# Top-k attention and a low-rank mixer: scales in one transfer a head, transposes of u two shares later, border work of batches 1 and 2 moved

## The chip, the cores and the metric

The kernel runs on one core of one Trainium2 chip. The metric is the device time of one execution in microseconds (us), the median over several. A core has five engines with queues of their own, each worked off in order: TensorE (PE, matrix products; its weight loads are listed as PEld), VectorE (DVE), ScalarE (ACT), GpSimd (POOL) and SyncE (SP). SP and ACT also issue the DMAs of this kernel; an issue holds the issuing queue.

## The reference

Eight batches, eight heads, 576 positions, 64 channels a head. For each head

```
scores = q k^T / 8                      (576 x 576)
keep the 32 largest of each row, softmax over them, x_head = attn v
x = heads side by side                  (576 x 512)
u = x + V^T U^T x     (mixing over the 576 positions, rank 32)
out = u + relu(u w1) w2                 (512 -> 2048 -> 512)
```

All is float32. U, V, w1 and w2 arrive as 64-bit numbers and are turned to 32 bits on the chip.

## The kernel before, in words

**Units of work.** Heads go in pairs `g` (four pairs a batch, 32 in all). The 576 query rows of a pair are four full tiles `t` = 0..3 of 128 rows, each with both heads side by side, and a tail tile `t` = 4 (`NT`) with 64 rows of each head on 128 partitions. A loop over steps `n` (L1182) takes one tile a step; from pair 4 (`NPAIR`, the first of batch 1 counted from 0, "batch 2" in the title's count) tile 3 and the tail share a step. Code before L1264 serves the first batch, the code from L1264 the other seven.

**A tile's way.** PE makes the scores (L336, L368), ACT copies them to SBUF (L381, L401, L404). To find the 32nd largest of a row, a tile is folded from pair 5 on: POOL adds the two halves as bits (L432), DVE takes the larger of each couple (L434, it reads one half straight from PSUM), POOL subtracts to get the smaller (L435). DVE then picks eights: L487 and L485 on the small half, L502, L515 and L520 on the large one. ACT and POOL turn everything under the threshold into a huge negative number (L546, L549, L550), ACT takes the exponential and its row sums `den` (L439, L560). From pair 6 DVE transposes in 32x32 blocks (L576), SP writes them to DRAM (`away`, L582), ACT issues the read back as `PT` (L591); earlier pairs, and all tails, are transposed on PE (L612, L617). PE multiplies with v (L688, L691, L662), ACT copies the result to `XT` (L700, L669), which has channels on partitions and positions along the row.

**The scales.** From pair 4 on the division by the row sums comes after that: `inverse` (L621) takes 1/`den` on DVE (L629, L631) and SP writes it to a DRAM tile `rd` of nine rows of 128 (L635): row 2t+h for tile t and head h, row 8 for the tail (64 of each head). `scale` (L639) reads it back spread over partitions, the 576 scales of head h on each of the 64 partitions of its half, with four DMAs a pair issued by ACT: per head one of 64x4x128 (L645) and one of 64x64 (L649). `mixed` (L703) then forms u = XT * scale on POOL: two products of 128x256 (L719) and one of 128x64 (L720).

**The mixing.** `mixed` is a generator, one stretch of which runs at each `fill()`. A step has eight such calls ("shares"). After the products it yields twice; PE then transposes u (four 128x128 at L725, the tail at L738) and ACT copies the result to `X` (L729, L739). It then waits until the next step has issued its values (L740 to L743), after which PE forms U^T x (L750), ACT copies (L758), PE multiplies with V (L762), ACT copies (L777), POOL adds to u (L778). The last pair is called with a fixed wait (`wait` = 5) instead. For pair 4 POOL also clears 64 rows of `X` (L736) here.

**The MLP.** `fill()` also takes from a queue of matmuls of the batch before, as many as a fixed share allows: L810 (first layer) with the ReLU copy L823 on ACT, L828 (second layer), then L839 on ACT and L840 on POOL, transposes L852, copies L854 and the store L858. The order on every engine is thus written down by the program; nothing is decided at run time.

**Parameters.** `next_params` (L218) brings in one block of weights a call: SP loads the raw words (L154), ACT makes three passes (L176, L177, L180), DVE one (L188), POOL two (L189, L191).

**The border.** Pair 4 is not folded, pair 5 is the first that is. The first fold's DVE and POOL part (`split`: L434, L435) was held back by `bound` until after the last selection of the step. Unfolded tiles write their first round of L515 to a `place`: for tiles of two heads a buffer with the tag `upper`, the tag that a fold's result uses too.

Of the kernel before, what the change touches and what calls it, by code (L numbers as in the profile page):

```python
# [26 lines left out]
def kernel(  # L27
# [106 lines left out]
    def at(t):  # L134
        return slice(OFF[t], OFF[t] + rows(t))

    def half(h):
        return slice(h * D, (h + 1) * D)
# [315 lines left out]
    def front(tiles):  # L454

        lanes = []
        for g, t in tiles:  # L460
            if t == 0:
                dens[g] = small.tile([P, 2 * NT + 1], F32, tag="den", name="den", bufs=3)
            S2, den = S2s.pop((g, t)), dens[g]
            early, pooled, gaps = ways(g, t)
            n = S2.shape[1]
            fold_of = folds.pop((g, t), None)
            for c in (1, 0) if n == 2 else (0,):
                slot = c if n == 2 or len(tiles) == 1 else 2
                lanes.append((
                    slot,  # L470
                    S2[:, c],
                    den[:, 2 * t + c : 2 * t + c + 1],
                    [a[:, c] for a in fold_of] if fold_of else None,
                    "early" if c in early else "pooled" if c in pooled else "gap" if c in gaps else "",
                ))
        W = len(lanes)
        first = small.tile([P, 3, 8], F32, tag="first", name="first", bufs=3)
        nmax = small.tile([P, 3], F32, tag="nmax", name="nmax", bufs=4)
        curs, places, ms = {}, {}, {}
        halves = [(lane[0], *lane[3]) for lane in lanes if lane[3]]  # L480
        for at_, step in ((0, 0), (0, 1), (8, 0)):
            for slot, upper, lower in halves:
                spot = upper[:, HALF + at_ : HALF + at_ + 8]
                if step:
                    nc.vector.match_replace(lower, spot, lower, NEG)  # L485
                else:
                    nc.vector.max(spot, lower)  # L487
        for slot, chunk, _, fold_of, _ in lanes:
            if fold_of:
                curs[slot] = fold_of[0]  # L490
            else:
                curs[slot] = chunk
                if slot == 2:
                    places[slot] = attn.tile([P, S], F32, tag="tplace", name="place", bufs=1)
                else:
                    places[slot] = attn.tile(
                        [P, 2, HALF + TOPK // 2], F32, tag="upper", name="upper"
                    ).rearrange("p c n -> p (c n)")[:, 0:S]
            ms[slot] = first[:, slot]
        order = [lane[0] for lane in lanes]  # L500
        for c in order:
            nc.vector.max(ms[c], curs[c])  # L502
        yield
        for i in range(1, TOPK // 8):
            if i == 1:
                nc.scalar.mul(nmax[:, 0:W], first[:, 0:W, 0], -SCALE)
                Es = {}
                for c, chunk, _, _, way in lanes:
                    if way == "early":
                        Es[c] = attn.tile([P, S], F32, tag="E", name="E")  # L510
                        weigh(chunk, Es[c], nmax[:, c : c + 1])
            for c in order:

                nxt = places.pop(c, curs[c])
                nc.vector.match_replace(nxt, ms[c], curs[c], NEG)  # L515
                curs[c] = nxt
            m8 = small.tile([P, 3, 8], F32, tag="m8", name="m8", bufs=4)
            for c in order:
                ms[c] = m8[:, c]
                nc.vector.max(ms[c], curs[c])  # L520
            yield
        for c, chunk, total, _, way in lanes:
            if way == "pooled":
                gap = attn.tile([P, S], F32, tag="E", name="E")
                nc.gpsimd.tensor_scalar(gap, chunk, ms[c][:, 7:8], NEG, ALU.is_lt, ALU.mult)
                nc.gpsimd.tensor_tensor(chunk, chunk, gap, ALU.add)  # L526
        for c, chunk, total, _, way in lanes:
            if way == "early":
                nc.vector.scalar_tensor_tensor(
                    out=chunk,  # L530
                    in0=chunk,
                    scalar=ms[c][:, 7:8],
                    in1=Es[c],
                    op0=ALU.is_ge,
                    op1=ALU.mult,
                    accum_out=total,
                )
        if t == NT:
            del qkTs[g]
        yield  # L540
        gaps = [lane for lane in lanes if lane[4] == "gap"]
        if gaps:
            slots = [lane[0] for lane in gaps]
            lo, hi = min(slots), max(slots) + 1
            least = small.tile([P, 3], F32, tag="least", name="least", bufs=3)
            nc.scalar.mul(least[:, lo:hi], m8[:, lo:hi, 7], WIDEN)  # L546
            for c, chunk, *_ in gaps:
                gap = attn.tile([P, S], F32, tag="E", name="E")
                nc.scalar.activation(gap, chunk, AF.Relu, bias=least[:, c : c + 1], scale=-WIDEN)  # L549
                nc.gpsimd.tensor_tensor(chunk, chunk, gap, ALU.subtract)  # L550
            yield
        rest = [lane for lane in lanes if lane[4] != "early"]
        if len(gaps) > 1:
            c, chunk, total, *_ = rest.pop(0)
            weigh(chunk, chunk, nmax[:, c : c + 1], total)
            yield
        for c, chunk, total, *_ in rest:
            weigh(chunk, chunk, nmax[:, c : c + 1], total)
        if t == NT and g != NPAIR - 1:
            nc.scalar.activation(den, den, AF.Identity, bias=eps)  # L560
        yield
# [77 lines left out]
    def scale(g):  # L639

        rd = scales.pop(g)
        sc = attn.tile([P, S], F32, tag="scale", name="scale", bufs=1)
        scales[g] = sc
        for h in range(2):
            nc.scalar.dma_start(  # L645
                sc[half(h), 0:MAIN].rearrange("p (t n) -> p t n", t=NT),
                rd[0 : 2 * NT].rearrange("(t h) n -> h t n", h=2)[h : h + 1].to_broadcast([D, NT, P]),
            )
            nc.scalar.dma_start(  # L649
                sc[half(h), MAIN:S], rd[2 * NT : 2 * NT + 1, half(h)].to_broadcast([D, TAIL])  # L650
            )

    def values(g, t):
# [49 lines left out]
    def mixed(g, wait, lag=0):  # L703
# [7 lines left out]
        uT = uTs[b][:, gi]  # L711
        if g >= NPAIR:
            sc = scales.pop(g)
            pairs_ = [
                a[:, 0:MAIN].rearrange("p (b n) -> p b n", b=2) for a in (XT, sc)
            ]
            ends = [uT[:, OFF[t] : OFF[t] + 2 * P] for t in (0, 2)]
            for i, end in enumerate(ends):
                nc.gpsimd.tensor_tensor(end, pairs_[0][:, i], pairs_[1][:, i], ALU.mult)  # L719
            nc.gpsimd.tensor_tensor(uT[:, at(NT)], XT[:, MAIN:S], sc[:, MAIN:S], ALU.mult)  # L720
            yield
            yield
        tp = ps_t.tile([P, NT, P], F32, tag="tp", name="tp")
        for t in range(NT):
            nc.tensor.transpose(  # L725
# [4 lines left out]
        if g < NPAIR:  # L730
            X4 = X4.rearrange("p t (h d) -> p t h d", h=2)
            den4 = den[:, 0 : 2 * NT].rearrange("p (t h) -> p t h ()", h=2)
            nc.gpsimd.tensor_tensor(X4, X4, den4.to_broadcast([P, NT, 2, D]), ALU.mult)
        else:
            if g == NPAIR:
                nc.gpsimd.memset(X[TAIL:P, NT, :], 0.0)  # L736
            tp = ps_t.tile([P, P], F32, tag="tp", name="tp")
            nc.tensor.transpose(tp[0:TAIL], uT[:, at(NT)], ident)  # L738
            nc.scalar.copy(X[0:TAIL, NT, :], tp[0:TAIL])  # L739
# [20 lines left out]
        for chunks, (lo, hi) in zip(PARTS, SPAN):  # L760
# [15 lines left out]
            else:  # L776
                nc.scalar.copy(sc[:, lo:hi], up[:, 0 : hi - lo])  # L777
                nc.gpsimd.tensor_tensor(uT[:, lo:hi], uT[:, lo:hi], sc[:, lo:hi], ALU.add)  # L778
            yield
        if gi == NPAIR - 1:  # L780
            fillers.append(closing(b) if b == B - 1 else mlp(b))

# [399 lines left out]
    for n in range(STEPS + 2):  # L1182
# [103 lines left out]
        if n < STEPS and n - 2 >= ALONE and len(tiles(n - 2)) > 1:  # L1286
            scale(steps[n - 2][0][0])
        next(here, None)
        next_params(1)
        fill()  # L1290
        if n >= STEPS:
            if n == STEPS:
# [1 line left out]
                scale(NP - 1)  # L1294
            weighted(n - 2)
        next(here, None)
        bound = tiles(n + 1)[:1] == [(NPAIR + 1, 0)]
        if not bound:
            for tile_ in tiles(n + 1):
                split(*tile_)  # L1300
        fill()
        next(here, None)
        if bound:
            for tile_ in tiles(n + 1):
                split(*tile_)
        for tile_ in tiles(n - 1):
            if shared(*tile_):
                blocks(*tile_)
# [5 lines left out]
                coming = loading(g + 2) if g + 2 < NP else iter(())  # L1314
            next(coming, None)
        next(ready, None)
        if t != 0:
            next_params(1)
        next(here, None)
        fill()  # L1320
# [36 lines left out]
```

## Time and profile before

| | |
|---|---|
| median of 3 runs | 1680.57 us (1680.2 to 1681.1) |
| the profiled execution | 1681.84 us, of which the span from first to last instruction is 1679.8 us |
| mean granted TensorE clock | 0.967 of full speed |
| busy: PE, DVE, ACT, POOL | 1571.6, 1547.1, 991.1, 1000.2 us |
| scale DMAs on ACT | 56 of 128 KB (L645, median 622 ns to issue) and 56 of 16 KB (L649, 627 ns) |
| products of u | 56 of 128x256 (L719, 740 ns), 28 of 128x64 (L720, 332 ns) |
| copies to X | 28 at L729 (586 ns), 28 at L739 (258 ns) |

How to read it: "busy" is time in which an engine executes, not time in which it decides the end. A wait row reads "engine line of the waiter <- engine line of the releaser: us in total, times, longest". In a timeline the columns are start, length, engine, line, operation and shape; a bracket gives the idle time before and who ended it. x counts instructions: a float32 matmul is two, a transpose one. Ends of matmuls are modelled, starts are not.

### The profile page before, as it was taken

The page shows a single profiled execution, that of the slowest core. Times are in us where ns is not written, and L with a number is a line of the kernel's source. Part 1 is how long each engine was busy: PE and PEld are TensorE (multiplying, and loading weights), DVE is VectorE, ACT ScalarE, POOL GpSimd, SP SyncE. Part 2 cuts the span into 40 slices and gives each one's busy share as a digit, 9 for nine tenths or more (in the row PEclk, how much of TensorE's full clock was granted, in tenths as well). Part 3 has the DMA queues.
Part 4 walks back from the last instruction along what each step waited for, and adds up shares of the span by engine and source line. Part 5 has one row for each costly group of instructions (what it writes and reads, how often), then busy time and mean ns, then how long its engine had stood idle before and what let it go on. Part 6 is the DMA issues. An engine that isn't in the chain of part 4 may idle for free.

```text
span 1679.8 us, 30303 instructions
## 1 busy us (share of the span) xinstructions
PE 1571.6 (94%) x9638; PEld 1183.9 (70%) x9638; DVE 1547.1 (92%) x4393; ACT 991.1 (59%) x2475; POOL 1000.2 (60%) x853
## 2 busy tenths in 40 slices
PE   4667698999899999999999999999999999999999
PEld 2444466687667786778777887778777887778776
DVE  7999998999999999999999999999999999994452
ACT  4888788665665556565655656565655656564320
POOL 4778668755666565666566565656666565653620
PEclk7787799999999999999999999999999999999999
DMA  3323232255555555555455455555555555543001
GB/s 87 94 76 97 62 94 73 63 135 132 134 128 135 127 142 132 139 127 138 121 134 137 124 146 132 137 128 136 126 130 136 126 149 132 131 120 110 10 1 28
DMA packets 295631, 189.42 MB, mean 113 GB/s; under 512 B 178768, under 2 KB 279984, under 8 KB 295472
## 3 DMA queue, kind: packets, MB, share of 16 engines
q1 hardware_dynamic: 259728, 117.62, 30.2%
q10 hardware_dynamic: 35744, 69.88, 13.7%
q8 instruction: 76, 1.25, 0.3%
q14 instruction: 83, 0.68, 0.1%
HBM read 116.49 MB, written 70.91 MB: 112 GB/s over the span
## 4 chain that ended last, share of the span: by engine, by line
PE 58%; DVE 25%; POOL 5%; DMA 4%; ACT 3%; issue 2%; SPq 2%; ACTq 0%; DVEq 0%; POOLq 0%
PE mm L828 17%; PE mm L810 16%; DVE m L520 7%; DVE upper L515 7%; PE sc L336 5%; PE O L691 5%; PE mm L904 3%; DVE first L502 2%; DVE y L576 2%; DVE upper L487 2%; PE sc L904 2%; PE tp L904 2%; DMA ld<-in_k_dram 2%; POOL uT L719 2%; PE up L762 1%
## 5 line engine op out<-in xcount | busy, mean ns | idle before, releaser
L550 POOL TENSOR_TENSOR Ssb<-Ssb,E 128x576 f32<-128x576 f32 x243 | 339.9, 1419 | 248.3 <-ACT E L549 247.8
L810 PE MATMUL mm<-uT,w 128*128 128x320 f32 (+1 forms) x1792 | 461.7, 410 | 2.4 <-ACT hT L823 2.0
L828 PE MATMUL mm<-hT,w 128*128 128x320 f32 (+1 forms) x1792 | 462.1, 407 | 0.0
L810 PEld LDWEIGHTS mm<-uT,w 128*128 128x128 f32 x1792 | 335.4, 191 | 103.0 <-issue 11.6
L828 PEld LDWEIGHTS mm<-hT,w 128*128 128x128 f32 x1792 | 332.3, 190 | 93.0 <-issue 10.2
L520 DVE MAX8 m<-upper 128x8 f32<-128x304 f32 (+1 forms) x780 | 367.3, 512 | 0.7
L515 DVE MATCH_REPLACE8 upper<-m,upper 128x304 f32<-128x304 f32 (+1 forms) x520 | 259.9, 507 | 0.0
L432 POOL TENSOR_TENSOR lower<-Ssb 128x576 uint32<-128x576 uint32 x108 | 152.6, 1413 | 139.1 <-ACT Ssb L381 52.2
L439 ACT ACTIVATE Ssb<-Ssb,nmax 128x576 f32<-128x576 f32 x258 | 201.4, 783 | 17.6 <-POOL Ssb L526 9.9
L435 POOL TENSOR_TENSOR lower<-lower,upper 128x576 uint32<-128x576 uint32 x108 | 153.1, 1418 | 74.2 <-DVE upper L434 72.6
L336 PE MATMUL sc<-qkT 64*128 64x288 f32 (+1 forms) x1056 | 179.0, 461 | 11.0 <-ACT Ssb L390 7.8
L487 DVE MAX8 upper<-lower 128x8 f32<-128x288 f32 x432 | 172.3, 440 | 10.7 <-POOL lower L435 10.7
L549 ACT ACTIVATE E<-Ssb,least 128x576 f32<-128x576 f32 x243 | 176.2, 769 | 4.2
L381 ACT COPY Ssb<-sc 128x576 f32<-128x576 f32 x216 | 127.6, 643 | 71.4 <-PE sc L336 71.4
L576 DVE STREAM_TRANSPOSE y<-Ssb 128x512 f32<-128x512 f32 (+1 forms) x312 | 153.9, 545 | 0.0
L823 ACT ACTIVATE hT<-mm 128x320 f32<-128x320 f32 (+1 forms) x224 | 91.9, 411 | 102.1 <-PE mm L810 100.9
L691 PE MATMUL O<-PT,va 128*64 128x128 f32 x2048 | 144.6, 285 | 0.0
L336 PEld LDWEIGHTS sc<-qkT 64*128 64x128 f32 (+1 forms) x1056 | 95.9, 197 | 51.7 <-issue 17.1
L691 PEld LDWEIGHTS O<-PT,va 128*64 128x64 f32 x2048 | 113.4, 141 | 16.4 <-issue 2.0
L700 ACT COPY XT<-O 128x128 f32<-128x128 f32 x128 | 33.8, 264 | 111.3 <-PE O L691 103.8
L515 DVE MATCH_REPLACE8 upper<-first,upper 128x304 f32<-128x304 f32 x216 | 97.7, 460 | 0.0
L485 DVE MATCH_REPLACE8 lower<-upper,lower 128x288 f32<-128x288 f32 x216 | 94.1, 444 | 0.0
(264 smaller groups left out, 2258.3 us busy)
## 6 DMA issues: line engine op xcount, KB each, us to landing
away<-y SPq DMA_DIRECT2D x416, 144.0 KB
PT<-away ACTq DMA_DIRECT2D x104, 576.0 KB
raw<-in_moe_w_ch_dram SPq DMA_DIRECT2D x32, 512.0 KB
va<-in_v_dram SPq DMA_DIRECT2D x64, 128.0 KB
out_dram<-ob SPq DMA_DIRECT2D x59, 128.0 KB
scale<-rd ACTq DMA_DIRECT2D x56, 128.0 KB
ld<-in_q_dram SPq DMA_DIRECT2D x108, 64.0 KB
ld<-in_k_dram SPq DMA_DIRECT2D x108, 64.0 KB
```

The lines of the kernel that those rows point to most:

```text
L336: nc.tensor.matmul(out, lhsT=qkT[half(h), 0, cols(t)], rhs=qkT[half(h), 1, lo:hi], start=True, stop=True,)
L435: nc.gpsimd.tensor_tensor(bottom, bottom, top.bitcast(U32), ALU.subtract)
L439: nc.scalar.activation(E, chunk, AF.Exp, bias=nmax, scale=SCALE, accum_out=total)
L487: nc.vector.max(spot, lower)
L515: nc.vector.match_replace(nxt, ms[c], curs[c], NEG)
L520: nc.vector.max(ms[c], curs[c])
L549: nc.scalar.activation(gap, chunk, AF.Relu, bias=least[:, c : c + 1], scale=-WIDEN)
L550: nc.gpsimd.tensor_tensor(chunk, chunk, gap, ALU.subtract)
L576: nc.vector.transpose(y[:, :, i * NT : i * NT + c].rearrange("p r c j -> p c r j"), E2[:, a : a + c * P].rearrange("p (c r j) -> p c r j", ...
L691: nc.tensor.matmul(O[half(h)], lhsT=va[:, h, j, :], rhs=PT[:, NT * h + j], start=False, stop=(j == NT - 1),)
L810: nc.tensor.matmul(ph[:, 0:w], lhsT=first_layer(cc, f), rhs=uT[:, cc, lo:hi], start=(cc == 0), stop=(cc == NC - 1),)
L828: nc.tensor.matmul(po[:, 0:w], lhsT=w2[:, f, c * P : (c + 1) * P], rhs=hTs[f][:, 0:w], start=(f == 0), stop=(f == NF - 1),)
```

## The change

1. **Scales.** `den` of pairs from 4 on is laid out head by head: column 5c+t for head c, so that columns 0 to 3 are head 0, column 4 the tail of both, 5 to 8 head 1. In `rd` the 576 scales of a head now lie in one run, those of head 1 from the middle of row 4. `scale` reads each with one DMA of 64 rows of 576 numbers: two DMAs a pair. The tile becomes 64 columns wider; head 0 has its tail behind, head 1 ahead, so the tail product is two of 64x64 on half the partitions each, in place of one of 128x64.
2. **Transposes.** After the products `mixed` yields four times, not twice, except for the last pair.
3. **Border.** `bound` goes; the first fold's second part stands at its usual place. The `place` buffers of that one step come from the idle tiles `scale` and `PTt`, not from `upper`. The call of `next_params` at that step goes, and one is added in the step of pair 5, tile 0. The clearing of 64 rows of `X` moves from pair 4's mixing to the end of pair 3's.

```diff
+                spot = CH * c + t if g >= NPAIR else 2 * t + c
-                    den[:, 2 * t + c : 2 * t + c + 1],
+                    den[:, spot : spot + 1],
...
+                elif (g, t) == (NPAIR, NT):
+                    places[slot] = attn.tile([P, TAIL + S], F32, tag="scale", name="place", bufs=1)[:, 0:S] if slot else (
+                        attn.tile([P, NT + 1, P], F32, tag="PTt", name="place", bufs=1)
+                    ).rearrange("p c n -> p (c n)")[:, 0:S]
...
-        sc = attn.tile([P, S], F32, tag="scale", name="scale", bufs=1)
+        sc = attn.tile([P, TAIL + S], F32, tag="scale", name="scale", bufs=1)
+        flat = rd.rearrange("r n -> () (r n)")
         for h in range(2):
             nc.scalar.dma_start(
-                sc[half(h), 0:MAIN].rearrange("p (t n) -> p t n", t=NT),
-                rd[0 : 2 * NT].rearrange("(t h) n -> h t n", h=2)[h : h + 1].to_broadcast([D, NT, P]),
-            )
-            nc.scalar.dma_start(
-                sc[half(h), MAIN:S], rd[2 * NT : 2 * NT + 1, half(h)].to_broadcast([D, TAIL])
+                sc[half(h), (1 - h) * TAIL : (1 - h) * TAIL + S],
+                flat[:, h * S : (h + 1) * S].to_broadcast([D, S]),
             )
...
-            nc.gpsimd.tensor_tensor(uT[:, at(NT)], XT[:, MAIN:S], sc[:, MAIN:S], ALU.mult)
-            yield
-            yield
+            for h in range(2):
+                a = (1 - h) * (TAIL + MAIN)
+                nc.gpsimd.tensor_tensor(
+                    uT[half(h), at(NT)], XT[half(h), MAIN:S], sc[half(h), a : a + TAIL], ALU.mult
+                )
+            for _ in range(4 if wait is None else 2):
+                yield
...
-            if g == NPAIR:
-                nc.gpsimd.memset(X[TAIL:P, NT, :], 0.0)
...
+        if g == NPAIR - 1:
+            nc.gpsimd.memset(X[TAIL:P, NT, :], 0.0)
...
-        next_params(1)
+        border = g == NPAIR and t == NT - 1
+        if not border:
+            next_params(1)
...
-        bound = tiles(n + 1)[:1] == [(NPAIR + 1, 0)]
-        if not bound:
-            for tile_ in tiles(n + 1):
-                split(*tile_)
+        for tile_ in tiles(n + 1):
+            split(*tile_)
         fill()
         next(here, None)
-        if bound:
-            for tile_ in tiles(n + 1):
-                split(*tile_)
...
-        if t != 0:
+        if t != 0 or g == NPAIR + 1:
             next_params(1)
```

More of the change, by code (lines that the diff above doesn't have):

```diff
@@ L713, in mixed @@
             sc = scales.pop(g)
-            pairs_ = [
-                a[:, 0:MAIN].rearrange("p (b n) -> p b n", b=2) for a in (XT, sc)
-            ]
+            main = sc[:, TAIL : TAIL + MAIN]
+            pairs_ = [a.rearrange("p (b n) -> p b n", b=2) for a in (XT[:, 0:MAIN], main)]
             ends = [uT[:, OFF[t] : OFF[t] + 2 * P] for t in (0, 2)]
```

## Prediction

> **What bounds the kernel now.** I read the busy time by windows first, cut at the period at which the timeline repeats (189.2 us, one batch), then the waits of DVE and PE, then timelines at the two places that these name.
>
> Busy time by windows (length, then busy and instructions of PE, PEld, DVE, ACT, POOL, then clock and DMA):
>
> ```profile
> core 0: us, PE busy (x) PEld busy (x) DVE busy (x) ACT busy (x) POOL busy (x), PEclk, DMA share, GB/s
> 741.93:931.13 189.20, 187.59 (x1189) 143.13 (x1189) 186.21 (x567) 112.25 (x286) 113.86 (x96) 1.00 0.54 133
> 336.00:552.73 216.73, 209.21 (x1322) 157.96 (x1321) 216.56 (x661) 129.92 (x331) 132.25 (x111) 0.98 0.53 133
> ```
>
> From 552 us to the last attention step at 1514 every batch looks like the first row: PE and DVE both nearly full. Between 336 and 552 (second row) DVE has 0.2 us idle in 217: there it alone sets the pace, and nothing that PE saves counts. ACT and POOL are at 60%.
>
> Waits of DVE, 336 to 1536 us:
>
> ```profile
> DVE upper L434 <- ACT Stail L401: 10.3, 9, 1.7
> DVE upper L487 <- POOL lower L435: 6.2, 7, 1.9
> ```
>
> These 16.5 us are nearly all that DVE loses in the stretch: each batch once 1.6 us at L434 and about 1.2 at L487. L401 copies scores that PE has just made, so the first row says that PE is late. PE waits for nothing there but the products of u:
>
> ```profile
> 756.66 0.44 PE L725 MATMUL tp<-ident,uT 128*128 128x128 f32 x2 [0.26 <-POOL uT L719]
> 757.35 0.44 PE L725 MATMUL tp<-ident,uT 128*128 128x128 f32 x2 [0.26 <-POOL uT L719]
> 757.63 0.30 PE L738 MATMUL tp<-ident,uT 128*64 128x128 f32 x1
> 757.78 2.54 PE L810 MATMUL mm<-uT,w 128*128 128x256 f32 x11
> ```
>
> That is PE's timeline at one pair. The last pair is one without the wait:
>
> ```profile
> 1551.29 0.60 PE L725 MATMUL tp<-ident,uT 128*128 128x128 f32 x4
> 1551.72 0.27 PE L738 MATMUL tp<-ident,uT 128*64 128x128 f32 x1
> 1551.83 2.54 PE L828 MATMUL mm<-hT,w 128*128 128x256 f32 x11
> ```
>
> From the first transpose to the next matmul it takes 0.54 us there and 1.12 here: 0.58 lost inside the group (ends are modelled, so the bracket shows less; starts count). Before it, twelve L810 from 753.55 last 3.11 us, where the last pair's eight take 1.84, 0.23 each: 0.35 more. The four pairs of this batch lose 0.93, 0.66, 0.97 and 0.98 in this way, **3.5 us a batch**. So PE needs 189.2 - 3.5 = 185.7 us a batch and DVE 186.2: PE bounds, and DVE is only 0.5 us behind it.
>
> The second wait of DVE, timeline of ACT, POOL and DVE:
>
> ```profile
> 790.65 0.62 ACTq L645 DMA_DIRECT2D scale<-rd  x1
> 791.31 0.63 ACTq L649 DMA_DIRECT2D scale<-rd  x1
> 791.97 0.62 ACTq L645 DMA_DIRECT2D scale<-rd  x1
> 792.63 0.62 ACTq L649 DMA_DIRECT2D scale<-rd  x1
> 793.30 0.20 ACT L506 ACTIVATE nmax<-first 128x2 f32<-128x2 f32 x1 [1.65 <-DVE m L520]
> 793.41 0.35 ACT L839 COPY oT<-mm 128x256 f32<-128x256 f32 x1
> 793.84 0.73 POOL L840 TENSOR_TENSOR oT<-oT,uT 128x256 f32<-128x256 f32 x1 [3.29 <-ACT oT L839]
> 794.53 1.42 POOL L435 TENSOR_TENSOR lower<-lower,upper 128x576 uint32<-128x576 uint32 x1
> 795.99 0.82 DVE L487 MAX8 upper<-lower 128x8 f32<-128x288 f32 x2 [0.96 <-POOL lower L435]
> ```
>
> Four issues hold ACT for 2.6 us; the copy L839 stands behind them, POOL's add L840 behind that, L435 behind it, and DVE waits. Around 602 us one issue lasts 1.54 us and the same chain costs DVE 1.85.
>
> **The change, part by part.** *Scales.* Two of four issues go: 1.31 us of ACT a pair (two at 0.62 to 0.63 and their spacing). In the chain above L839 could start at 792.1 (its matmuls end at 792.2), 1.2 us earlier, more than the 0.96 waited; at 602 us, without the third and fourth issue, about 2.1, more than 1.85. So the L487 waits go: **-6.2**. What an issue of 64 rows of 2304 bytes costs is not in the trace: below by the read of `PT` (L591, 128 rows of 4608 bytes, 0.33 us), above by L645's 0.62; I take 0.62. Its landing has cover: the last scale packet of the issues from 743.4 ends at 748.3, and L719 begins at 755.87, so 7.6 us later would still do. The Trainium skill (Perfetto Trace Analysis, DMA Optimizations) speaks against merging: split transfers may let work start sooner. With 7.6 us to spare that is worth nothing here, and by that rule too the sum would stay. The tail product becomes two: at most 2 x 0.33 for 0.33 on POOL (below, two of half the cost, nothing); L435 follows directly, ends at 758.95, and L487 takes its result at 759.76, so 0.33 fits in 0.8; without that cover it would be 0.33 x 28 = 9 us.
>
> *Transposes.* In PE's order they move three or four matmuls down (two instructions each, 0.22 us at 256 columns, 0.27 at 320), some 1.65 us past the place where they would start unhindered. At 756.66 that place is 756.31, so 757.96. L719 ends its second product at 757.25, the tail products end by 757.9, and the tail is transposed 0.44 after the first: all is there, with 0.4 us to spare. Group and copies end 0.7 us later than now, since the waits inside go. What is queued behind the copies on ACT: L546 and L549 of the same step, then L550 on POOL. In the tightest of the four pairs (804 us) ACT afterwards idles 3.88 us and POOL 4.16, which hides 0.7. On PE two matmuls (1.08 us) follow before the next user of the same PSUM buffer in one pair in four (L852), against a copy of 0.59: covered, else 0.5 a batch. L750 keeps its place. So PE gets 3.5 us a batch, and the L434 waits go: **-10.3**. What is late next: DVE itself. Its need of 186.2 stands 0.5 above PE's, and two engines that close hinder each other; `PT` is no obstacle, as L688 comes 6 to 9 us after its issue here and 4.5 to 5 where DVE set the pace without a loss. I leave **+5** (1 us a batch; ends 0, and 9, half of PE's saving).
>
> *Border.* Timeline of DVE, waits only:
>
> ```profile
> 250.24 0.82 DVE L487 MAX8 upper<-lower 128x8 f32<-128x288 f32 x2 [1.31 <-POOL lower L435]
> 261.98 0.21 DVE L629 RECIPROCAL upright<-den 128x9 f32<-128x9 f32 x1 [2.19 <-ACT den L560]
> 275.03 0.43 DVE L188 TENSOR_SCALAR w<-w 128x512 uint32<-128x512 uint32 x1 [2.80 <-ACT w L176]
> 289.55 0.82 DVE L487 MAX8 upper<-lower 128x8 f32<-128x288 f32 x2 [2.94 <-POOL lower L435]
> ```
>
> L434 moves ahead of three L515 and three L520 (4.2 us), so POOL, idle for 6.3 us there, has L435 done long before L487: 1.31 goes. PE's wait of 2.17 us for L434 at 248.66 goes too. One L188 (1.14 us) moves from 238 to behind L631, into the slack before the next L487. But L629 waits for a chain over L550, L439 and L560 that starts at the last L520, and that comes only some 0.4 us sooner; with one parameter's two POOL passes (2.6 us) out of its way I count 1.7 at 262. At 275 ACT is behind the four scale issues: 1.3 more. The 2.94 stays, as POOL and DVE move together. **-3.0**, from 0 (the chain does not move) to -4.9 (the 1.9 us at L434 at 331 goes as well). The cleared rows: POOL now waits for pair 3's last use (L766, done about 209.8) in front of an L189 that ran at 207.23; the next use of POOL is at 214.07 after 4.18 us idle, and the block whose load SP issues behind it (209.92) is first read at 218.86. Free; without cover 2.6. The later parameter block has 29 us to its first use. The clock: in the windows 248.3 to 251.7 and 425.8 to 432.6 the granted clock is 0.50, after PE idled 2.17 and 3.08 us. The Trainium skill (TensorE: Matmul & The Clock Gate, What's actually happening) has half clock only after an idle window of about 3.4 us, so by it the shorter wait would cost no clock. By the rows both did; but DVE sets the pace at both, so I add nothing for it.
>
> *Sum.* -3.0 - 6.2 - 10.3 + 5 = -14.5 against the profiled execution's 1681.84 us: 1667.3. The median was 1.27 lower, so **1666 us**.
>
> **Rivals.** (a) *Half of it*: the transposes still meet a late product (POOL's queue slides with ACT's), or PE meets a new wait, and only L487 and the border's 1.3 at the scale issues remain: 7.5, giving 1673. For it: the margin is 0.4 us. (b) *No change*: PE's wait moves into waiting for `PT` or for L434, and DVE's into another of POOL's results; 0 to 3 us, 1680. Against it: the windows 336 to 552, where DVE ran without such waits. (c) *Slower*: copies L729 and L739 reach ACT 0.7 us later and delay L546, L549, L550 and so POOL's L435 in each of 28 pairs: 28 x 0.7 = 19.6, less 6.2 and 3.0, is +10, 1691. It decides once L435 is more than 0.8 us late (759.76 against 758.95). Against it: L435 stands ahead of L550 in that step, and the idle times above.
>
> **How the numbers follow.** Forecast 0.62, (a) 0.20, (b) 0.10, (c) 0.08. Faster by over 0.2% (3.4 us, about what a measurement of this kernel tells from no change): 0.82; within: 0.10; slower: 0.08. Low end: all waits go, 4.9 + 16.5 + 1.27 off 1681.84, 1659. High end: (a) with no gain at the border, 6.2 off, 1674, and 2 for what (a) leaves open: 1676.
>
> **What would show it.** Right: per-batch period near 186.5 to 187.5 us; no PE wait at the transposes, their group 0.54 us long; DVE's L434 and L487 rows near zero; two issues a pair. Wrong: PE waiting at L688 or L336, ACT idle before L729 with DVE waits at L487 growing, an issue of 64 rows that takes over 1.2 us, or scale packets that end after L719 could start.

## The result and the profile after

The changed kernel takes **1663.03 us** (median of 4 runs, 1662.32 to 1664.24) against 1680.38 for the kernel before (4 runs): ratio 0.9897, interval 0.988 to 0.9914. It is faster, as forecast, and 3 us below the forecast of 1666. The profiled execution took 1662.32 us, its span 1660.2. Lines after the change are up to six higher: L434 keeps its number; L487, L550, L591, L688, L719, L720, L725, L738 and L810 are now L488, L555, L596, L691, L721, L724, L731, L742 and L816.

First the busy time by windows, cut where the first transpose of u of every fourth pair starts, so one row is one batch (columns as before):

```profile
core 0: us, PE busy (x) PEld busy (x) DVE busy (x) ACT busy (x) POOL busy (x), PEclk, DMA share, GB/s
750.60:936.80 186.20, 185.78 (x1189) 143.69 (x1188) 185.89 (x565) 113.06 (x284) 115.15 (x100) 1.00 0.54 135
936.80:1122.31 185.51, 185.51 (x1189) 143.76 (x1188) 185.37 (x565) 112.94 (x284) 115.21 (x100) 1.00 0.54 136
```

A batch takes 185.5 to 186.2 us where it took 189.2. PE and DVE are both busy for all but 0.4 us of it. The waits of DVE from 336 to 1516, where the last attention step starts, are now one row; L434 has none:

```profile
DVE upper L488 <- POOL lower L435: 0.5, 2, 0.3
```

PE's timeline at the pair that stood at 756 us before, and ACT's at the scale issues that stood at 790:

```profile
750.60 0.60 PE L731 MATMUL tp<-ident,uT 128*128 128x128 f32 x4
...
751.14 2.54 PE L816 MATMUL mm<-uT,w 128*128 128x256 f32 x11
```

```profile
783.19 1.18 ACTq L651 DMA_DIRECT2D scale<-rd  x2
...
784.56 0.37 ACT L845 COPY oT<-mm 128x256 f32<-128x256 f32 x1
```

The transposes' group is 0.54 us long, without a bracket. The issues end 1.2 us after they began, and the copy L845 starts 0.2 us later.

At the border, DVE's waits from 210 to 336 us:

```profile
...
DVE upper L434 <- ACT Stail L401: 1.9, 1, 1.9
DVE upper L488 <- POOL lower L435: 1.8, 2, 1.3
```

With L634 (2.2 us) and L188 (1.9), 7.8 us in all, where the same window held 11.4 before. The L434 that ends the border starts at 329.07 instead of 331.27: 2.2 us gained there. From it to the reciprocal of the last pair (1536.50 before, 1516.35 now) 17.95 more are gained, and behind that, where PE alone works until the end, 0.55 is lost. How the 17.95 divide show these two rows, of before and of after:

```profile
331.27:1536.50 1205.23, 1186.53 (x7513) 905.41 (x7512) 1180.98 (x3577) 715.41 (x1813) 723.39 (x611) 1.00 0.53 132
```

```profile
329.07:1516.35 1187.28, 1177.50 (x7515) 908.76 (x7513) 1179.10 (x3576) 719.88 (x1814) 732.12 (x637) 1.00 0.54 134
```

DVE's idle time falls from 24.25 to 8.18 us, 16.1 less; the other 1.9 is DVE's busy time, for the same instructions but one; why they take less is not shown.

### The profile page after: what moved, and what is told of

Its sections match the earlier page's. It is cut to its first block, busy times and chain, and to the rows that moved or that the text cites. A ratio compares the mean times of both kernels' runs of the same rounds, so it can differ in the third digit from the quotient of the medians.

```text
span 1660.2 us, 30248 instructions
## 1 busy us (share of the span) xinstructions
PE 1555.9 (94%) x9638; PEld 1183.2 (71%) x9638; DVE 1547.4 (93%) x4393; ACT 995.1 (60%) x2475; POOL 1009.4 (61%) x881
## 4 chain that ended last, share of the span: by engine, by line
PE 66%; DVE 25%; DMA 4%; SPq 1%; issue 1%; ACT 1%; POOL 1%; DVEq 0%; ACTq 0%; POOLq 0%
PE mm L834 21%; PE mm L816 19%; DVE m L525 8%; DVE upper L520 7%; PE sc L336 6%; PE O L694 5%; PE mm L910 3%; DVE first L507 3%; PE tp L910 2%; PE sc L910 2%; PE sc L368 2%; DMA PT<-away 2%; PE up L766 1%; DVE y L581 1%; DVE upper L488 1%; DVE place L520 1%
## 5 line engine op out<-in xcount | busy, mean ns | idle before, releaser
L816 PE MATMUL mm<-uT,w 128*128 128x320 f32 (+1 forms) x1792 | 459.8, 409 | 1.2 <-ACT hT L829 1.0
L555 POOL TENSOR_TENSOR Ssb<-Ssb,E 128x576 f32<-128x576 f32 x243 | 340.0, 1419 | 185.4 <-ACT E L554 185.2
L816 PEld LDWEIGHTS mm<-uT,w 128*128 128x128 f32 x1792 | 334.1, 190 | 100.7 <-issue 10.6
L525 DVE MAX8 m<-upper 128x8 f32<-128x304 f32 (+1 forms) x774 | 362.5, 509 | 0.7
L520 DVE MATCH_REPLACE8 upper<-m,upper 128x304 f32<-128x304 f32 (+1 forms) x516 | 256.6, 504 | 0.0
L435 POOL TENSOR_TENSOR lower<-lower,upper 128x576 uint32<-128x576 uint32 x108 | 152.5, 1412 | 141.7 <-DVE upper L434 137.2
L439 ACT ACTIVATE Ssb<-Ssb,nmax 128x576 f32<-128x576 f32 x258 | 201.8, 784 | 28.8 <-POOL Ssb L531 10.3
L554 ACT ACTIVATE E<-Ssb,least 128x576 f32<-128x576 f32 x243 | 176.3, 769 | 4.2
L488 DVE MAX8 upper<-lower 128x8 f32<-128x288 f32 x432 | 171.8, 438 | 2.3 <-POOL lower L435 2.3
L520 DVE MATCH_REPLACE8 upper<-first,upper 128x304 f32<-128x304 f32 x216 | 97.5, 458 | 0.0
L507 DVE MAX8 first<-upper 128x8 f32<-128x304 f32 x216 | 90.1, 458 | 0.0
```

What stands on the lines that cost most here:

```text
L435: nc.gpsimd.tensor_tensor(bottom, bottom, top.bitcast(U32), ALU.subtract)
L439: nc.scalar.activation(E, chunk, AF.Exp, bias=nmax, scale=SCALE, accum_out=total)
L816: nc.tensor.matmul(ph[:, 0:w], lhsT=first_layer(cc, f), rhs=uT[:, cc, lo:hi], start=(cc == 0), stop=(cc == NC - 1),)
```

## The theories and the experiments

**Theory S** is that of the prediction's sum: a wait is worth its own length, so the parts add up. **Theory N** is its rival: PE sets the pace, the scales' part alone gives nothing, and only the transposes' part brings the batch down to 186. The first four runs take the change apart. Each was timed beside the kernel before. Between these series the median of the kernel before moved from 1680.4 to at most 1682.0 us, so a difference between medians of two series is good to about 2 us.

### The scales' part alone

The edit in short:

```diff
-  main: 64x4x128 (L645) and tail: 64x64 (L649), per head
+  sc[half(h), (1 - h) * TAIL : (1 - h) * TAIL + S] <- flat[:, h * S : (h + 1) * S]
-  one tail product of 128x64
+  two tail products of 64x64
```

> The kernel before with the scales' part alone: two issues a pair in place of four, the tail product of u in two. Theory N (PE sets the pace at 189.2 us a batch through its waits at the transposes of u, and a wait of DVE that goes is given back at L434 while PE stays late): the waits at DVE's MAX8 for POOL's L435 go (6.2 us between 336 and 1536), those at L434 grow from 10.3 to about 15, the period of a batch stays near 189; only the border's L188 gains, so 1679 (0 to -2.5 us). Theory S (each wait is worth its own length, as the prediction's sum had it): the MAX8 waits go and L434's stay at 10.3, so -6.2 and -1.3 at the border: 1673.

Measured: 1688.36 us, ratio 1.0037 (1.0025 to 1.0049): **slower by 7 us**, which neither theory had. One batch, and PE's timeline at a pair:

```profile
757.03:947.58 190.55, 188.03 (x1188) 143.21 (x1188) 186.70 (x565) 112.87 (x285) 115.09 (x101) 1.00 0.53 132
```

```profile
757.03 0.44 PE L727 MATMUL tp<-ident,uT 128*128 128x128 f32 x2 [0.26 <-POOL uT L717]
...
758.39 0.30 PE L740 MATMUL tp<-ident,uT 128*64 128x128 f32 x1 [0.23 <-POOL uT L720]
758.52 0.81 PE L812 MATMUL mm<-uT,w 128*128 128x256 f32 x3
```

The second bracket is new. The tail product is now two, 0.32 us each (half the partitions cost as much as all of them, 0.33), and the tail's transpose waits for the second. The group takes 1.49 us (1.12 before). Counted over the four pairs of this batch as in the prediction, from starts, PE loses 5.0 us instead of 3.5; 190.55 - 5.0 = 185.5, the same need of PE as in the kernel before. So N was right that PE sets the pace, and the missing term is 1.5 us a batch. DVE's waits at L434 grow to 20.5 us in the whole run (12.1 before): what is gained at the MAX8 comes back there, and more.

### The transposes' part alone

```diff
-            yield
-            yield
+            for _ in range(4 if wait is None else 2):
+                yield
```

> The kernel before with the transposes of u two shares later, nothing else. Theory N: PE's loss of 3.5 us a batch goes, the L434 waits of DVE (10.3 us) go, those at the MAX8 for L435 (6.2) stay, since the four issues on ACT stay: -10, 1670, period of a batch about 187.3. Theory S gives the same number for this run. A rival, that the later copies on ACT push L435 back, has MAX8's waits growing from 6.2 to over 9 and the gain at 6 or less: 1674 or more.

Measured: 1685.84 us, ratio 1.0026 (1.0013 to 1.0039), with a spread of 1677.6 to 1691.7 over 12 runs. The forecast of 1670 was wrong too, and so was the rival's mechanism: DVE's waits for L435 are 7.6 us between 336 and 1540, not over 9. PE waits at no transposes (each steady group 0.55 us), yet the batches of the profiled execution, its fastest at 1677.59, are uneven. What the slower executions lost stands in no trace. This batch takes 190.8 us, the next 187.0:

```profile
757.55:948.34 190.79, 188.19 (x1189) 144.37 (x1188) 185.95 (x565) 112.31 (x284) 113.75 (x97) 0.99 0.53 132
```

ACT's timeline in it, with the third and the fourth issue:

```profile
929.33 0.33 ACTq L591 DMA_DIRECT2D PT<-away  x1
...
931.50 0.62 ACTq L645 DMA_DIRECT2D scale<-rd  x1
934.28 0.47 ACTq L649 DMA_DIRECT2D scale<-rd  x1
934.80 0.20 ACT L506 ACTIVATE nmax<-first 128x2 f32<-128x2 f32 x1 [3.96 <-DVE m L520]
```

Between the third issue's end (932.12) and the fourth's start lie 2.16 us in which ACT does nothing. The bracket names DVE's L520, but L506 reads `first`, which L502 had made by 928.7; at other pairs the same wait is put down to L576, to L515 or to SP. The hold itself is seen only in the starts of the issues. The read of `PT` issued at 929.33 was still moving packets in this queue until 933.4. Behind the fourth issue stand the copy L823, for which PE's L810 waits 2.6 us, and then the scores and L434, for which DVE waits 3.1. Counted over 21 pairs from 550 to 1520 us, the fourth issue was held for over 0.2 us in 6 pairs of the kernel before (9.3 us in all) and in 17 here (23.5 us): the scale issues come 1.07 us after the issue of `PT` on the mean, before 1.37. In the kernel before, the six held pairs are exactly those in which that distance is under 1 us (0.59 to 0.95; the others 1.22 to 2.43). Here it is not the whole condition: a pair at 2.29 was held, one at 0.58 was not.

### The border's part alone, and all but the transposes

```diff
 border alone: before, with the change's lines of bound, place, next_params and memset
 all but the transposes: after, with
-            for _ in range(4 if wait is None else 2):
-                yield
+            yield
+            yield
```

> The kernel before with the border's part alone: first fold, parameter and clearing moved. From the trace of the changed kernel, DVE reaches the last wait at the border 2.2 us earlier than before, of which about 1.1 at L188 comes by the scales' part. So theory B (the border's own part works alone): -1 to -2, 1679. Rival (its gain needs the scales' part, since POOL and DVE wait behind the four issues there): 0, 1680.4. A loss would show as a new wait of POOL in front of the moved clearing.

> The changed kernel with the transposes of u at their old place: scales and border as changed. Theory N: PE still loses some 3.5 us a batch, the period stays near 189, so only the border's 2.2 and up to 1.5 more are gained: 1677 (1676 to 1679). Theory S: the scales' 6.2 and the border's 2.2: 1672.

Measured: the border alone 1681.33, ratio 0.9999 (0.9988 to 1.001), not told from no change; its L434 at the border starts at 329.85 (331.27 before), so 1.4 us show in the trace and nothing of it in the time, which scatters from 1678.7 to 1687.5. All but the transposes: 1686.97, ratio 1.0027 (1.0016 to 1.0039), with the group of 1.5 us and the period of 190.5 of the scales alone. Both theories missed it by the same second tail product.

### Four issues and three issues

So each large part alone loses, and together they gain 17. The next theory: the scales' part is needed because of the hold, and the transposes' part covers the second tail product. What makes the hold, the number of pieces a transfer is cut into or the number of issues? The edits in short:

```diff
 four: both heads; three: head 1 only
-                sc[half(h), (1 - h) * TAIL : (1 - h) * TAIL + S], flat[:, h * S : (h + 1) * S]
+                two transfers of 288 scales each
```

> The changed kernel, but each head's 576 scales in two transfers of 288: four issues a pair again, in the new layout, so 64 rows of 1152 bytes each (256 rows a pair; the kernel before has 640 pieces, of 512 and 256 bytes). In the profile of the transposes alone the four issues took 2.71 to 5.76 us (mean 3.75), with ACT held up to 2.9 us between the third and the fourth while the packets of the read of PT and of the first issues were still under way; in the changed kernel the two take 1.24 to 1.8. Theory P (the hold comes from the number of pieces outstanding): four issues take 2.5 to 2.8 each time, no hold; DVE's waits at the MAX8 for L435 come back as before, some 1 us a batch: 1667 to 1670. Rival I (the hold comes from the number of issues): the block takes up to 5 us again, and the time goes to that of the transposes alone, 1678 to 1690, with a wide spread.

> The changed kernel with head 1's scales in two transfers, so three issues a pair. With four issues, only the fourth was ever held (by 1.4 to 3.0 us in most pairs of that run), while the read of PT issued some 0.9 us ahead of the first was still under way. Theory F (a fifth transfer in the queue, behind PT and three of scales, is what is held): three issues take 1.9 us each time, no hold, time 1663 to 1665. Rival G (each further issue costs its share): half of the way to four issues, about 1675.

Measured: four issues 1688.27 us, ratio 1.0041 (1.0028 to 1.0053), so **25 us above the changed kernel, for two more issues a pair**; three issues 1664.92, ratio 0.9892 (0.988 to 0.9905), not to be told from the changed kernel's 0.9897. ACT's timeline with four:

```profile
931.92 0.33 ACTq L596 DMA_DIRECT2D PT<-away  x1
...
932.76 0.47 ACTq L653 DMA_DIRECT2D scale<-rd  x1
...
933.26 4.75 ACTq L653 DMA_DIRECT2D scale<-rd  x3
938.06 0.20 ACT L511 ACTIVATE nmax<-first 128x2 f32<-128x2 f32 x1 [4.62 <-DMA PT<-away]
```

Three issues that take 0.6 each last 4.75. Here the bracket names the read of `PT`, whose last packet ends at 936.71; the fourth issue starts at 937.56. With 256 rows in place of 640 pieces the fourth is held in 20 of 21 pairs (40.4 us in all), with three issues never, and the block takes 1.79 us. ACT's timeline with three:

```profile
923.02 0.47 ACTq L652 DMA_DIRECT2D scale<-rd  x1
...
923.52 0.61 ACTq L652 DMA_DIRECT2D scale<-rd  x1
...
924.17 0.62 ACTq L652 DMA_DIRECT2D scale<-rd  x1
```

So it is the number of issues that stand behind one another in the queue (theories I and F right, P and G wrong). Pieces and bytes are ruled out as the limit: in the old layout the third issue went in without a hold in every pair behind 320 pieces, where the held fourth of four stands behind 192; and the third of three goes in behind as many bytes (216 KB) as the held fourth of four. That the queue waits for the read of `PT` is argued from the times only: in the 20 held pairs the fourth issue starts 0.6 to 1.5 us after that read's last packet, but in the 21st it went in at 1507.63, 1.0 us ahead of it.

The waits that follow are, from 336 to 1540 us, PE's at L818 for the copy L831 behind the issues (17.4 us, up to 3.2), DVE's at L434 (14.6, up to 5.0) and DVE's at L488 for L435 (10.0, up to 2.3; 0.5 in the changed kernel).

### One share and four shares later

```diff
-            for _ in range(4 if wait is None else 2):
+            for _ in range(3 if wait is None else 2):      (one share later)
+            for _ in range(6 if wait is None else 2):      (four shares later)
```

> The changed kernel with the transposes one share later than before instead of two. Theory N: PE's loss at a pair's transposes (1.3 us at the old place with two tail products) falls by the one or two matmuls put in front of them, to 0.4 to 0.8 us, a period of about 187.5 in place of 186.0, so 1668 to 1677. Rival (margin: one share is enough, what is left fits into PE's own slack of 0.3 us a batch): 1662 to 1665.

> The changed kernel with the transposes of u four shares later than before instead of two. Theory N (PE's losses at the transposes are gone already, DVE sets the pace): no more to gain, 1662 to 1664, the transposes' group at 0.55 us, new waits at most where the copies L733 and L743 come later. Rival (c) of the prediction (the later copies on ACT push L551 and then L435): waits of DVE at L488 grow by 0.5 to 1 us a pair, 1676 or more.

Measured: one share 1667.94, ratio 0.9919 (0.9906 to 0.9933); four shares 1671.2, ratio 0.994 (0.9927 to 0.9952). Two shares lie between two losses. With one share, PE's timeline still meets the tail product:

```profile
940.36 0.30 PE L742 MATMUL tp<-ident,uT 128*64 128x128 f32 x1 [0.24 <-POOL uT L724]
```

With four, the transposes themselves are clean, but the next user of their PSUM buffer comes too soon behind them. PE, then ACT:

```profile
945.78 0.49 PE L691 MATMUL O<-PT,vd 128*128 128x128 f32 x2 [0.67 <-ACT x L735]
```

```profile
943.82 1.44 ACT L554 ACTIVATE E<-Ssb,least 128x576 f32<-128x576 f32 x2
945.17 0.56 ACT L735 COPY x<-tp 128x512 f32<-128x512 f32 x1
```

The copy L735 now stands behind the 1.44 us of L554, and PE's product O, which takes the buffer next, waits 0.67 and, in another pair of the batch, 0.50. Both kernels run a period of 187.2 us: with one share the four groups of a batch take 3.9 us in place of 2.2; with four, PE is busy for 186.05 us and waits for these 1.17. Theory N's "no more to gain" was wrong for four shares, and rival (c)'s mechanism did not come either: DVE's waits for L435 are 2.3 us between 336 and 1540 (0.5 in the changed kernel), not 0.5 to 1 a pair.

### Without the border, and without the scales

The changed kernel with one part taken back each time (its hunks as in the change).

> The scales' part and the transposes' part together, without the border's part. Theory N: the period of 186 is kept; what is lost is the border's 2.2 us, 1665. Rival (the border alone measured 0.9999 of before, so its part is worth nothing): 1663.

> The changed kernel without the scales' part: four issues in the old layout, transposes two shares later, border as changed. By the runs so far: no PE wait at the transposes, the fourth issue held in most pairs, period 186.5 to 191 and uneven, 1680 to 1688 with a wide spread, as the transposes alone. Rival (the border's part was what was missing beside the transposes): below 1675.

Measured: without the border 1665.52, ratio 0.9905 (0.9891 to 0.9919), 2.5 us more by the medians and within the interval of the changed kernel; its L434 at the border starts at 332.94, 3.9 later than in the changed kernel. Without the scales 1681.7, ratio 0.9996 (0.9984 to 1.0008), 1675.9 to 1686.8 over 12 runs: the fourth issue held in 16 of 21 pairs (28.8 us), as expected. So the border's part is not what the transposes' part lacked.

### Fillers earlier

The one version that could have beaten the changed kernel: the MLP's matmuls spread with 0.95 or 1.0 in place of 0.91.

```diff
-    SLOTS, LONG, EARLY = 8, 1.4, 0.91
+    SLOTS, LONG, EARLY = 8, 1.4, 0.95      (second kernel: 1.0)
```

> The changed kernel with the constant that spreads the fillers (the matmuls of the MLP) over the shares at 0.95 in place of 0.91, so that they run somewhat earlier. After the last attention step PE alone works until the closing (DVE waits 23.1 us for the last product); fillers that are done earlier shorten that. Up to 4 us: 1659 to 1663. Rival: where PE and DVE are 0.3 us apart a batch, earlier fillers make PE late for the scores, L434 waits again, 1664 or more.

> The same with 1.0 in place of 0.91: either more of the same gain (1658 to 1662), or the rival: L434's waits come back in every batch, 1666 or more.

Measured: 1663.8, ratio 0.9883 (0.9868 to 0.9897), and 1664.73, ratio 0.9892 (0.9879 to 0.9905): the same as the changed kernel. Neither expectation came: no gain to be told from the scatter, and L434's waits stay at 0.3 and 0.6 us. With 0.95 DVE's last wait, for the last product of u, ends at 1544.25 (1542.05 in the changed kernel): DVE's last L634 starts 1.1 us later (1517.48 against 1516.35), and behind it, after a wait of 1.97 us for `PT` at L691, PE runs at half clock from 1518.98 to 1522.39, where the changed kernel keeps full clock after one of 2.00. PE's timeline there, with 0.95:

```profile
1518.79 0.65 PE L691 MATMUL O<-PT,vd 128*128 128x128 f32 x2 [1.97 <-DMA PT<-away]
1519.37 1.98 PE L694 MATMUL O<-PT,va 128*64 128x128 f32 x16
```

The same sixteen matmuls take 1.09 us in the changed kernel. PE's waits at L691 also grow in total (6.4 us in the changed kernel from 336 to 1540, 8.9 and 13.4 here), but most of it is one wait near 415 us (5.95 and 6.13), in the stretch where DVE sets the pace. Whether the earlier fillers gain anything without that is not settled.

## Why the prediction was right, and where its steps failed

**The bound.** Right, and now shown twice: 189.2 less 3.5 gave 185.7 for PE, 190.55 less 5.0 gave 185.5, and with the waits gone a batch takes 185.5 to 186.2.

**Transposes, -10.3.** The L434 waits between 336 and 1536 went, as forecast, and the margin of 0.4 us behind the late product held in every steady pair (0.42 to 0.97 from the end of the second tail product to the tail's transpose); the run with one share shows that half of the shift would not have been enough. At 423.64 one wait of 3.1 us for L721 stays, in the stretch where DVE sets the pace.

**Scales, -6.2.** The waits went (0.5 left), but the working was wrong in two prices. "Two of four issues go: 1.31 us of ACT a pair" counted the issues as if each took its 0.62. From the first issue's start to the last one's end, the block of the kernel before took 3.08 us on the mean, since the fourth issue was held in 6 of 21 pairs, and now takes 1.16: 1.9 a pair. The long issue at 602 us that the prediction mentions is something else: there the third issue itself took 1.54 us and the fourth was not held, and the changed kernel, with two issues, has one of 1.15 at 597.22. Its cause is open. And the second tail product was weighed only against L435, "0.33 fits in 0.8". In front of the tail's transpose, with the transposes at their old place, it costs PE 1.5 us a batch, which made the part alone a loss of 7 us. The Trainium skill (Perfetto Trace Analysis, DMA Optimizations) says that splitting DMAs into smaller chunks may allow some to start sooner, and expects an earlier end of the whole task from it where the DMA engines are generally idle. Here their mean busy share was 0.54 in a batch, and splitting two transfers into four cost 25 us.

**The sum.** As an account of the parts, this is the step that failed: -3.0 - 6.2 - 10.3 + 5 adds the parts as if each brought its own wait. By the runs the parts alone are worth +7.0 (scales), +4.5 (transposes) and 0 (border) by their medians, and together -17.35. In the pair, taking the transposes back costs 23.9 us (1686.97 - 1663.03) and taking the scales back 18.7 (1681.7 - 1663.03). The sum came out near because both parts were there, each covering what the other exposes. The prediction had checked that the later transposes clear both tail products, but not that the scales' part loses without them; and of the hold, which only the scales' part keeps away from the later transposes, it did not know. That this cover was there was luck; for either part alone the same sum would have been wrong in sign. Without the +5 the three parts add up to -19.5, the very difference of the two profiled executions: DVE's waits add up where all of them go, which is no price for each.

**+5 for two engines that are close.** Mis-sized: the term should have been 0.5. DVE waits for 0.5 us between 336 and 1516 in all, though PE and DVE need the same time within 0.4 us a batch. That is 4.5 us of the 5.0 by which the two profiled executions differ from the sum (-19.5 against -14.5). DVE's shorter busy time is 1.9 more, which no step had; 0.8 at the border and 0.55 at the end stand against them. So the period, too, came out at 185.5 to 186.2, below the 186.5 to 187.5 that the prediction named as a sign of being right.

**Border, -3.0.** Measured -2.2 at L434 near 329. The wait of 1.31 at 250 went and L188 lost 1.1, as expected; L629's wait of 2.2 and the 1.9 at L434 stayed; the wait of 2.94, expected to stay, fell to 1.31. Waits up to there fell by 4.1 us, but DVE's busy time in the stretch grew by 1.9 (109.85 to 111.77 us). Timed without the border, the difference is inside the intervals.

**Rivals.** (a), half of it, did not come: nothing was late by the margin. (c) did not come: in every run with the later transposes and at most three issues, DVE's waits for L435 between 336 and 1540 are 2.3 us or less, against 6.2 before. What made the parts alone slower was neither. For the scales it was the second tail product. For the transposes the runs point to the hold in ACT's queue, which the trace of before showed in 6 of 21 pairs and which the prediction did not look for.

## What to carry to other kernels

Two waits that show in one profile aren't two independent prices: ask for each part alone what it exposes, since a cover that one part gives may be what the other needs. Read the starts of consecutive DMA issues, not their lengths alone: here a gap between two issues of one queue was a hold, whatever the bracket behind it named, and it came more often when the issues followed an earlier transfer more closely. When an instruction is moved, try distances on both sides: here too little met its producer, too much its buffer's next user.

## What was not expected of the hardware

- Behind a read of 128 rows of 4608 bytes in ACT's queue, three further issues went in at 0.46 to 0.69 us each on the mean, and the fourth was held up to 3.0 us; with 64 rows of 1152 bytes it was held at least as often (20 of 21 pairs) as with pieces of 512 (16 and 17, transposes later). Why the queue takes three is not shown by these runs, nor why some fourth issues pass.
- The kernels with the four issues of the old layout and transposes that do not wait scatter by 14.1 us (1677.6 to 1691.7) and 10.9 us over 12 runs; the kernel before, in the series of the second, by 6.9 over 17; the changed kernel by 1.9 over 4.
- A GpSimd product of 64x64 took 0.32 us on 64 partitions, one of 128x64 took 0.33.
- After idle times of PE that hardly differ the granted clock stayed at 1.0 once (2.00 us, the changed kernel at 1517.69) and fell to 0.50 twice (1.97 and 2.04 us, with the fillers earlier).
- In the run with four issues PE's waits brought a stretch of half clock into the steady batches (0.50 from 937.74 to 944.57), which is not there in the changed kernel.
